# Attention and two expert layers on one core: mask added by TensorE, and three engines' order written by hand for the first two batches

## The chip, the cores and the metric

The kernel runs on one core of a Trainium2 chip. Times are device microseconds of one execution of the whole program. Of two times of this kernel that differ by under 0.3% (5.7 us) the measurement cannot say which is lower.

## What is computed

Three layers follow one another. Attention has 4 batches, 8 heads, 576 positions and head size 64; the first four heads see a band of 32 positions, the other four every fourth position of a band of 128. The second layer takes the larger of three products, and the third mixes eight experts with weights from a Sinkhorn iteration.

```
scores = scale * np.matmul(q, k.transpose(0, 1, 3, 2))
scores = np.where(masks[None, :, :, :], scores, -1000000000.0)
scores = scores - np.max(scores, axis=-1, keepdims=True)
attn = np.exp(scores)
attn = attn / (np.sum(attn, axis=-1, keepdims=True) + 1e-09)
x = np.matmul(attn, v)                      # then reshaped to (2304, 512)
h = np.maximum(np.maximum(x @ w1, x @ w2), x @ w3)
x = h @ w_out                               # second layer, d_ff 768
# third layer: 8 experts, each relu(x @ w1[e]) @ w2[e], weighted by P[:, e]
```

## The kernel before

**Work in units.** The second layer is computed batch by batch (b = 0 to 3) in tiles f of 128 hidden columns. One unit is 12 matmuls of 128x288 into one PSUM bank of a ring of four. A tile has six units: for each half of the batch's 576 positions the three products w1, w2, w3. After the first, ScalarE copies PSUM to `tmp`; after the second, VectorE takes the maximum with `tmp`; after the third it takes the maximum again, ScalarE writes the rounded half of `h` and VectorE the rest (a subtraction). Every product is done as three passes over such halves. The list `WORK` gives the order of tiles: batch 0's first five, then tiles 4 and 5 of batches 0 and 1 in turn (units 0 to 47), then `0.out`, the projection back (units 48 to 55), and so on. `hooks(unit)` is called after each unit and issues what goes beside it.

**Attention.** The four head pairs p of batch 0 come first, alone, by a list of steps, `ORDER`. A step's first letter says what it is: S scores (TensorE), M the mask and the maximum (VectorE), X the exponentials (ScalarE), R the reciprocal (VectorE) and the scaling with it (GpSimd), T transposes and E their evacuation, V the product with v, H and L the two halves of the result `xt`. `L290` is L, `L192` and `L200` are M. The pairs of batch 1 run beside units 0 to 29 of batch 0 (`BEGIN`, `STAGES`), those of batch 2 beside units 43 to 87.

**Weights' conversion.** The second layer's weights come as 64-bit floats and are turned to 32 bits by nine steps, c1 to c9 (`narrow_ops`): VectorE does c1, c3, c4, c6, c7 and c9, ScalarE c2, c5 and c8. Two chunks of 128x512 make a group g; c1 to c7 of a group are one instruction of 128x1024 each, c8 and c9 two of 128x512. Chunk j belongs to tile j // 3. Groups 0 and 1 are converted within the first part, groups 2 to 8 as the tiles need them, and groups 9 to 11 (the projection's) beside tiles 4 and 5.

**Who sets the order.** TensorE's instructions run in the order of the code throughout. On ScalarE, VectorE and GpSimd the list `ORDER` fixes the first part; from there to `1.out` the framework's scheduler orders them by its own estimates, so that several groups' steps may be interleaved; from `1.out` on ScalarE's and VectorE's order is the code's again. An engine runs its queue strictly in order: an instruction that waits holds all behind it.

Of the kernel before, what the change touches and what calls it, by code (L numbers as in the profile page):

```python
# [30 lines left out]
WEIGHTS = 78  # L31
# [14 lines left out]
FUSED = "1010"  # L46
EVAC = "AAV VAA VAV AAA".split()
ORDER = (
# [52 lines left out]
def attention_moe(ctx: ExitStack, tc: tile.TileContext, q, k, v, mask, wm1, wg, wm2, out):  # L101
# [27 lines left out]
    mk = at_p.tile([P, BANK0 + NQ * KW], F32, name="mk", bufs=1)  # L129
# [21 lines left out]
    def attn_ops(b, p, pool, qt, kt, vt, fused, evac):  # L151
# [12 lines left out]
        def s():  # L164
            if b == 0 and p % 2:
                h["s"] = [ps_g.tile([P, 512], F32, name="ps") for _ in range(2)]
            else:
                h["s"] = [ps_a.tile([P, 512], F32, name=f"pss{a}", bufs=1) for a in range(2)]

            for i in range(T0 if corners else 0):  # L170
                for a, (t0, t1) in enumerate(halves):
                    t = t0 + i
                    for j in range(2 if t < t1 else 0):
# [4 lines left out]
                            start=True, stop=True,  # L178
                        )
            for t in range(0 if corners else NQ):  # L180
# [3 lines left out]
                    start=True, stop=True,  # L184
                )

        def ma():
            h["m"] = pool.tile([P, NQ, KW], F32, name="sm", bufs=2 if pool is at_p else 3)
            for a, (t0, t1) in enumerate(halves):
                n = (t1 - t0) * KW  # L190
                m0 = BANK0 + t0 * KW if dil else a * KW
# [6 lines left out]
        def mb():  # L198
            h["st"] = pool.tile([P, 3, NQ], F32, name="st")
            nc.vector.tensor_reduce(out=h["st"][:, 0], in_=h["m"], axis=AX.X, op=ALU.max, negate=True)  # L200

        def xs():
            if not fused:
                nc.gpsimd.tensor_tensor(
                    out=h["m"], in0=h["m"], in1=h["st"][:, 0].unsqueeze(2).to_broadcast([P, NQ, KW]),
                    op=ALU.add,
                )

        def xe():
# [150 lines left out]
    def load_w1(b, g):  # L360
# [11 lines left out]
        if g < NG:  # L372
            nc.sync.dma_start(wm1f[g], raw)
# [1149 lines left out]
```

## Time and profile before

| | us |
|---|---|
| median of three runs | 1898.76 |
| lowest and highest | 1896.23, 1902.53 |
| the profiled execution's own time | 1901.93 |
| its span in the profile | 1899.9 |
| TensorE busy in the span | 1853.2 (98%) |
| VectorE, ScalarE, GpSimd busy | 1341.1, 976.6, 651.3 |

A share of the whole span says little here, since the change touches only the first fifth of it, up to about 342 us. Line numbers are those of the kernel before; `PE` is TensorE, `DVE` VectorE, `ACT` ScalarE, `POOL` GpSimd.

### The profile page before, as it was taken

What the parts mean: (1) busy time and instruction counts of PE and PEld (TensorE: products, weight loads), DVE (VectorE), ACT (ScalarE), POOL (GpSimd) and SP (SyncE); (2) the same over time, 40 slices, a digit from 0 to 9 for tenths busy, and PEclk for the clock granted to TensorE, in tenths of its full rate; (3) what the DMA queues carried; (4) which work ended last, traced back from release to release, by engine and by line L of the source; (5) the groups of instructions that cost most, each with busy time, mean ns of one, the idle gap of its engine ahead of it and who ended that gap; (6) DMA issues with size and microseconds to landing.
All of it is one profiled execution on the core that took longest, in us unless ns stands there. A gap on an engine that the chain in (4) does not pass through costs nothing.

```text
span 1899.9 us, 34083 instructions
## 1 busy us (share of the span) xinstructions
PE 1853.2 (98%) x12051; PEld 1745.9 (92%) x12051; DVE 1341.1 (71%) x2529; ACT 976.6 (51%) x2362; POOL 651.3 (34%) x553
## 2 busy tenths in 40 slices
PE   7899999999999999999999999999999999999998
PEld 6899999998899987999999999999989999999997
DVE  7983364677866667666677777777777677876777
ACT  5663445444554444444456555565545555555554
POOL 2123243335666667666612121121211111211111
PEclk7899999999999999999999999999999999999999
DMA  7766486866667678766977767777798676676763
GB/s 262 277 217 222 151 274 202 304 226 228 237 252 259 252 252 291 263 254 250 363 257 235 237 218 225 239 233 237 232 331 262 211 233 225 225 255 212 234 219 100
DMA packets 218488, 458.81 MB, mean 241 GB/s; under 512 B 19920, under 2 KB 102992, under 8 KB 216784
## 3 DMA queue, kind: packets, MB, share of 16 engines
q1 hardware_dynamic: 216688, 454.29, 70.2%
q10 hardware_dynamic: 1632, 2.36, 0.4%
q8 instruction: 95, 1.56, 0.3%
q14 instruction: 73, 0.60, 0.1%
HBM read 325.76 MB, written 130.81 MB: 240 GB/s over the span
## 4 chain that ended last, share of the span: by engine, by line
PE 83%; DVE 8%; DMA 4%; ACT 2%; issue 1%; POOL 1%; DVEq 0%; SPq 0%; ACTq 0%; POOLq 0%
PE po L1292 25%; PE po L1387 12%; PE po L1037 10%; PE ps L419 7%; PE p L1387 6%; PE q L1387 6%; PE q L1083 4%; PE p L1083 4%; PE ps L629 4%; DMA raw<-in_wm 1%; PE ps L549 1%; DVE sums L771 1%; PE q L549 1%; DVE h L1135 1%; DVE ts L810 1%
## 5 line engine op out<-in xcount | busy, mean ns | idle before, releaser
L1292 PE MATMUL po<-wt,hop 128*128 128x256 f32 (+1 forms) x3264 | 482.9, 310 | 2.8 <-DMA wt<-wtd 2.8
L1292 PEld LDWEIGHTS po<-wt,hop 128*128 128x128 f32 x3264 | 444.9, 191 | 38.5 <-ACT wt L83 3.0
L84 POOL TENSOR_TENSOR wt<-raw,wt 128x256 fp32r<-128x256 f32 x192 | 186.2, 994 | 757.9 <-ACT wt L83 746.9
L84 DVE TENSOR_TENSOR hop<-r,hop 128x384 fp32r<-128x384 f32 x384 | 208.9, 574 | 188.3 <-ACT hop L83 184.7
L1037 PE MATMUL po<-wb,h 128*128 128x512 f32 x1152 | 295.2, 392 | 0.4 <-POOL wb L84 0.4
L1037 PEld LDWEIGHTS po<-wb,h 128*128 128x128 f32 x1152 | 213.6, 188 | 34.3 <-POOL wb L84 1.2
L83 ACT CAST hop<-r 128x384 fp32r<-128x384 f32 x384 | 188.7, 516 | 55.7 <-DVE r L1268 30.8
L419 PE MATMUL ps<-xt,wa 128*128 128x288 f32 x1296 | 187.7, 301 | 4.6 <-DVE wa L323 2.0
L419 PEld LDWEIGHTS ps<-xt,wa 128*128 128x128 f32 x1296 | 176.9, 191 | 8.2 <-DVE wa L323 2.3
L84 POOL TENSOR_TENSOR wa<-raw,wa 128x256 fp32r<-128x256 f32 (+1 forms) x107 | 129.8, 1217 | 111.9 <-ACT wa L83 91.0
L1401 ACT ACTIVATE r<-r 128x384 f32<-128x384 f32 x192 | 99.8, 525 | 128.9 <-DVE r L1400 128.0
L84 POOL TENSOR_TENSOR tw<-ts,tw 128x512 fp32r<-128x512 f32 x64 | 85.3, 1354 | 93.5 <-DVE h L1135 57.4
L1387 PE MATMUL po<-xB,wa 128*128 128x384 f32 x576 | 116.9, 338 | 0.0
L1387 PE MATMUL po<-xt,wa 128*128 128x384 f32 x576 | 116.9, 338 | 0.0
L1321 DVE SCALAR_TENSOR_TENSOR acc<-po,prob,acc 128x256 f32<-128x256 f32 x222 | 95.1, 476 | 21.9 <-PE po L1292 17.5
L84 POOL TENSOR_TENSOR wa<-sums,wa 128x512 fp32r<-128x512 f32 x64 | 88.7, 1404 | 53.3 <-ACT wa L83 28.4
L84 POOL TENSOR_TENSOR wb<-raw,wb 128x512 fp32r<-128x512 f32 x64 | 93.2, 1456 | 29.2 <-ACT wb L83 28.8
L1387 PEld LDWEIGHTS po<-xB,wa 128*128 128x128 f32 x576 | 102.5, 188 | 0.0
L1387 PEld LDWEIGHTS po<-xt,wa 128*128 128x128 f32 x576 | 102.5, 188 | 0.0
L1262 DVE TENSOR_TENSOR r<-r,r 128x384 f32<-128x384 f32 x128 | 93.1, 728 | 2.2
L771 DVE TENSOR_TENSOR sums<-raw 128x256 f32<-128x256 f32 x64 | 41.4, 646 | 71.1 <-DMA raw<-in_wm 71.1
L1303 ACT COPY mm<-po 128x256 f32<-128x256 f32 x144 | 49.6, 375 | 79.9 <-PE po L1292 79.9
(236 smaller groups left out, 3364.7 us busy)
## 6 DMA issues: line engine op xcount, KB each, us to landing
wa<-wsd SPq DMA_DIRECT2D x192, 512.0 KB, 4.4
wt<-wtd SPq DMA_DIRECT2D x256, 256.0 KB, 3.9
wsd<-wa SPq DMA_DIRECT2D x96, 512.0 KB, 3.4
raw<-in_wm SPq DMA_DIRECT2D x64, 512.0 KB, 4.3
wtd<-tw SPq DMA_DIRECT2D x128, 256.0 KB, 2.8
raw<-in_wm SPq DMA_DIRECT2D x128, 256.0 KB, 5.4
wa<-wsd SPq DMA_DIRECT2D x64, 256.0 KB, 4.7
cx<-in_wm SPq DMA_DIRECT2D x12, 1024.0 KB, 6.8
```

The costliest lines, as they stand in the source:

```text
L83: nc.scalar.copy(hi, src)
L84: sub.tensor_tensor(out=lo, in0=src, in1=hi.bitcast(F32), op=ALU.subtract)
L419: nc.tensor.matmul(ps, w[:, wi, kk], xt[:, xi, kk, n0:n0 + HB], start=(n == 0), stop=(n == 3 * KT - 1),)
L629: nc.tensor.matmul(ps, wo[f][:, wi, d2 * P:(d2 + 1) * P], hs[f][:, hi, a * HB:(a + 1) * HB], start=(f == 0 and n == 0), stop=(f == NF1 - 1 ...
L771: nc.vector.tensor_tensor(out=s[:, o], in0=x, in1=y, op=op)
L1037: nc.tensor.matmul(po, self.hs[f, j][:, hi, t * P:(t + 1) * P], self.ws[f][:, wi], start=(n + f + k == 0), stop=(n == NPAIR - 1 and f == 1 ...
L1083: nc.tensor.matmul(ps, wo[w][:, wi, kk], xo[x][:, xi, kk], start=(first and k == 0), stop=True if k == 5 else False, skip_group_check=not ...
L1262: nc.vector.tensor_tensor(out=r[o, n], in0=r[x, n], in1=r[y, n], op=op)
L1292: nc.tensor.matmul(self.ps[side, t][:, 0:x.shape[-1]], h[:, hi, t * P:(t + 1) * P], x, start=(first and i == 0), stop=(n == NPAIR - 1 and ...
L1321: nc.vector.scalar_tensor_tensor(out=a, in0=src, scalar=g, in1=a, op0=ALU.mult, op1=ALU.add)
L1387: nc.tensor.matmul(ps[k][side], wo[k][w][:, wi, kk], xo[x][:, xi, kk], start=(first and c == 0), stop=c == 5, skip_group_check=not first,)
L1401: nc.scalar.activation(out=r, in_=r, func=AF.Relu)
```

## The change

In batches 0 and 1 a matmul writes the mask into PSUM first (`eyes`, an identity scaled by 8, times the mask's 64 rows), and the scores are added to it there. VectorE then takes only the maximum, straight from PSUM, and the exponentials read PSUM, with the scale and the maximum in the same instruction. Two pairs of batch 0 that had one long exponential with a subtraction on GpSimd and a sum on VectorE now have nine with their own sums, as the others. The first part has a new order of loads and steps and converts four chunks.

From there to `1.out` the scheduler no longer orders ScalarE, VectorE and GpSimd (`first.enter_context`): their queues hold what the code issues, unit by unit. A group's conversion is issued in four pieces beside four units, from the units in `NARROW` on: c1 c2, then c3 c4 c5, then c6 c7 c8, then c9. Batch 1's weights are split as batch 2's were, two units a chunk. Batch 1's and 2's attention steps are spread by new tables.

```diff
-OUTER = {"0.4": (0, 1), "0.5": (2,)}
-BEGIN = {1: (0, 5, 10, 16), 2: (43, 60, 67, 73), 3: (91, 98, 105, 112)}
+BEGIN = {1: (0, 6, 12, 17), 2: (43, 59, 66, 72), 3: (91, 98, 105, 112)}
-STAGES = {0: "S Ma Mb Xs Xe Xb Ra Rb", 6: "W", 8: "T0 E0 T1 E1", 9: "T2 E2", 11: "V0 H0 L0 V1 H1 L1"}
-LOADS = "k0 m0 k1 k2 m2 k3 v0 g0 v1 g1 v2 v3"
+SECOND = {
+    0: "S M", 1: "X0", 2: "X1", 3: "X2", 4: "X3 X4", 5: "Ra Rb", 6: "W",
+    8: "T0 E0 T1 E1", 9: "T2 E2", 10: "V0 H0", 11: "V1 H1 L0", 12: "L1",
+}
+NARROW = (0, 4, 8, 13, 17, 21, 25, 29, 33, 37)
+WEIGHTS = {1: 46, 2: 78}
+LOADS = "m0 k0 g0 w0 k1 m2 k2 k3 v0 g1 v1 v2 v3 g2"
-EVAC = "AAV VAA VAV AAA".split()
+EVAC = "VVV VVA AVA AVA".split()
...
+            for a, (t0, t1) in enumerate(halves if b < 2 else ()):
+                n, m0 = (t1 - t0) * KW, mask_at(a)
+                nc.tensor.matmul(
+                    h["s"][a][:, 0:n], eyes, mr[:QT, m0:m0 + n], start=True, stop=False, skip_group_check=True,
+                )
...
+        def m():
+            weights()
+            for a, (t0, t1) in enumerate(halves):
+                nc.vector.tensor_reduce(
+                    out=h["st"][:, 0, t0:t1],
+                    in_=h["s"][a][:, 0:(t1 - t0) * KW].rearrange("p (t k) -> p t k", k=KW),
+                    axis=AX.X, op=ALU.max, negate=True,
+                )
+            nc.vector.tensor_scalar_mul(h["st"][:, 0], h["st"][:, 0], 1.0 / D ** 0.5)
...
+    def narrow(g, step):
+
+        raw, ops = narrowing[g]
+        for name in ("c1 c2", "c3 c4 c5", "c6 c7", "")[step].split():
+            ops[name]()
+        if step == 2:
+            ws = [w1_tile(g) for _ in range(2)]
+            (made[0] if g < NG else wo).extend(ws)
+            parts = [(ws[i], raw[:, i]) for i in range(2)]
+            narrowing[g] = raw, parts
+            for w, x in parts:
+                nc.scalar.copy(w[:, 0], x)
+        if step == 3:
+            for w, x in ops:
+                nc.vector.tensor_tensor(out=w[:, 1], in0=x, in1=w[:, 0].bitcast(F32), op=ALU.subtract)
+            if g < NG:
+                nc.sync.dma_start(wm1f[g], raw)
...
+        for g, u in enumerate(NARROW, 2):
+            if 0 <= unit - u < 4:
+                narrow(g, unit - u)
+            if unit == max(u - 5, 0) and g > 2:
+                fetch_narrow(g)
...
+    first.enter_context(tc.manual_schedule(engines={EN.Activation, EN.DVE, EN.Pool}))
...
         if what == "1.out":
-            ordered.enter_context(tc.manual_schedule(engines={mybir.EngineType.Activation, mybir.EngineType.DVE}))
+            first.close()
+            ordered.enter_context(tc.manual_schedule(engines={EN.Activation, EN.DVE}))
```

Two places show what moves. The first is VectorE's queue where batch 0's first part ends and unit 0 follows; before, from the last products of attention on (L290 is L, L323 to L341 are conversion steps: L326 c1, L331 c3, L334 c4, L338 c6, L341 c7, L323 c9; numbers are those of buffers).

```order
L290 TENSOR_TENSOR xt_101<-ps_439,xt_101 128x112
L290 TENSOR_TENSOR xt_101<-ps_439,xt_101 128x144
L323 TENSOR_TENSOR wa_155<-raw_137,wa_155 128x512
L338 SCALAR_TENSOR_TENSOR cx_664<-cx_664 128x1024
L331 SCALAR_TENSOR_TENSOR raw_856<-cx_857,raw_856 128x1024
L323 TENSOR_TENSOR wa_478<-raw_137,wa_478 128x512
L341 TENSOR_TENSOR raw_663<-raw_663,cx_664 128x1024
L334 TENSOR_SCALAR cx_857<-cx_857 128x1024
```

After the change the same place of VectorE's queue (L305 is L; L214 and L219 are M of batch 1's first pair; L458 the maximum of unit 1; L347, L350, L354, L357 are c3, c4, c6, c7 of group 2, whose c1 stands further up):

```order
L305 TENSOR_TENSOR xt_105<-ps_479,xt_105 128x32
L214 TENSOR_REDUCE st_568<-pss0_545 128x5
L214 TENSOR_REDUCE st_568<-pss1_546 128x4
L219 TENSOR_SCALAR st_568<-st_568 128x9
L458 TENSOR_TENSOR tmp_521<-ps_572,tmp_521 128x288
L347 SCALAR_TENSOR_TENSOR raw_150<-cx_151,raw_150 128x1024
L350 TENSOR_SCALAR cx_151<-cx_151 128x1024
```

Groups 2 and 3 stood there interleaved with L; now M and a maximum stand ahead of group 2. The second place is VectorE's queue in the middle of batch 0's units, before (two and three groups at a time: buffers 873, 1064, 1220):

```order
L338 SCALAR_TENSOR_TENSOR cx_874<-cx_874 128x1024
L192 SCALAR_TENSOR_TENSOR sm_646<-pss1_627,mk_100 128x384
L192 SCALAR_TENSOR_TENSOR sm_646<-pss0_626,mk_100 128x480
L331 SCALAR_TENSOR_TENSOR raw_1064<-cx_1065,raw_1064 128x1024
L84 TENSOR_TENSOR h1_490<-ps_606,h1_490 128x288
L341 TENSOR_TENSOR raw_873<-raw_873,cx_874 128x1024
L326 TENSOR_SCALAR raw_1220<-cx_1221 128x1024
L200 TENSOR_REDUCE st_649<-sm_646 128x9
```

After the change VectorE's queue beside units 33 to 36, group 10 whole and the first step of group 11 (L343 c1, L398 c9, L463 the subtraction of a third unit):

```order
L343 TENSOR_SCALAR raw_1414<-cx_1415 128x1024
L458 TENSOR_TENSOR tmp_1511<-ps_1528,tmp_1511 128x288
L347 SCALAR_TENSOR_TENSOR raw_1414<-cx_1415,raw_1414 128x1024
L350 TENSOR_SCALAR cx_1415<-cx_1415 128x1024
L458 TENSOR_TENSOR ps_1545<-ps_1545,tmp_1511 128x288
L354 SCALAR_TENSOR_TENSOR cx_1415<-cx_1415 128x1024
L357 TENSOR_TENSOR raw_1414<-raw_1414,cx_1415 128x1024
L463 TENSOR_TENSOR hx_1451<-ps_1545,hx_1451 128x288
L398 TENSOR_TENSOR wb1_1562<-raw_1414,wb1_1562 128x512
L398 TENSOR_TENSOR wb1_1563<-raw_1414,wb1_1563 128x512
L458 TENSOR_TENSOR tmp_1568<-ps_1585,tmp_1568 128x288
L343 TENSOR_SCALAR raw_1507<-cx_1508 128x1024
```

One group is finished there before the next begins, and one operation of a unit stands between two steps.

## Rows read from the trace of the kernel before

**Rows 1.** Stretch, length, busy us (instructions) by engine; then clock, DMA share, GB/s.

```profile
0.00:47.50 47.50, 33.95 (x293) 29.73 (x293) 37.60 (x70) 27.12 (x77) 12.93 (x14) 0.78 0.77 262
47.50:118.70 71.20, 62.12 (x650) 58.32 (x649) 69.41 (x108) 50.19 (x144) 8.34 (x4) 0.93 0.71 255
118.70:151.90 33.20, 33.20 (x279) 32.71 (x277) 24.79 (x44) 16.69 (x49) 9.02 (x6) 1.00 0.71 247
151.90:342.40 190.50, 188.27 (x1816) 182.80 (x1816) 90.29 (x185) 84.68 (x282) 66.47 (x57) 1.00 0.64 211
```

**Rows 2.** TensorE in order of time: start, length, line, tiles, count, idle before.

```profile
47.50 1.86 PE L175 MATMUL pss<-kt,qt 64*64 64x96 f32 x36
...
118.68 25.70 PE L419 MATMUL ps<-xt,wa 128*128 128x288 f32 x192
144.31 1.04 PE L175 MATMUL pss<-kt,qt 64*64 64x96 f32 x36
...
151.87 3.31 PE L629 MATMUL ps<-h,wb 128*128 128x288 f32 x23
```

**Rows 3.** VectorE's groups by shape, 47.5 to 118.7 us: busy us, mean ns.

```profile
L338 DVE SCALAR_TENSOR_TENSOR cx<-cx 128x1024 f32<-128x1024 uint32 x8 | 11.9, 1487 | 0.2 <-ACT cx L337 0.2
L341 DVE TENSOR_TENSOR raw<-raw,cx 128x1024 f32<-128x1024 f32 x8 | 11.1, 1391 | 0.0
L323 DVE TENSOR_TENSOR wa<-raw,wa 128x512 fp32r<-128x512 f32 x15 | 9.9, 678 | 0.0
L331 DVE SCALAR_TENSOR_TENSOR raw<-cx,raw 128x1024 uint32<-128x1024 uint32 x8 | 9.7, 1211 | 0.0
L334 DVE TENSOR_SCALAR cx<-cx 128x1024 uint32<-128x1024 uint32 x8 | 5.5, 686 | 0.0
...
L200 DVE TENSOR_REDUCE st<-sm 128x9 f32<-128x864 f32 x4 | 4.2, 1042 | 0.0
...
L192 DVE SCALAR_TENSOR_TENSOR sm<-pss,mk 128x480 f32<-128x480 f32 x4 | 2.6, 644 | 0.0
L192 DVE SCALAR_TENSOR_TENSOR sm<-pss,mk 128x384 f32<-128x384 f32 x4 | 2.1, 534 | 0.0
...
L234 DVE TENSOR_SCALAR st<-st 128x9 f32<-128x9 f32 x4 | 0.7, 164 | 1.6 <-ACT sm L215 1.6
```

**Rows 4.** ScalarE's groups by shape in the same stretch.

```profile
L319 ACT CAST wa<-raw 128x512 fp32r<-128x512 f32 x15 | 8.6, 620 | 6.1 <-DVE raw L341 6.0
L337 ACT ACTIVATE cx<-cx 128x1024 f32<-128x1024 uint32 x7 | 8.2, 1173 | 0.0
L330 ACT ACTIVATE raw<-raw,ebias 128x1024 uint32<-128x1024 uint32 x7 | 8.2, 1165 | 0.1
```

**Rows 5.** VectorE in order of time, first steps of group 11.

```profile
132.06 0.68 DVE L326 TENSOR_SCALAR raw<-cx 128x1024 uint32<-128x1024 uint32 x1
132.66 0.45 DVE L84 TENSOR_TENSOR hx<-ps,hx 128x288 fp32r<-128x288 f32 x1
133.96 1.23 DVE L331 SCALAR_TENSOR_TENSOR raw<-cx,raw 128x1024 uint32<-128x1024 uint32 x1 [0.85 <-ACT raw L330]
```

**Rows 6.** VectorE in order of time, the first mask step, and conversion at 77 us.

```profile
7.07 0.66 DVE L192 SCALAR_TENSOR_TENSOR sm<-pss,mk 128x480 f32<-128x480 f32 x1 [6.07 <-PE pss L181]
...
77.18 1.22 DVE L338 SCALAR_TENSOR_TENSOR cx<-cx 128x1024 f32<-128x1024 uint32 x1
...
80.28 2.65 DVE L341 TENSOR_TENSOR raw<-raw,cx 128x1024 f32<-128x1024 f32 x1
```

**Rows 7.** GpSimd in order of time, one of four scalings between 60 and 112 us.

```profile
79.45 2.40 POOL L238 TENSOR_TENSOR sm<-sm,st 128x864 f32<-128x864 f32 x1 [15.24 <-ACT h L83]
```

**Rows 8.** Busy time and granted clock, three short stretches.

```profile
40.70:50.00 9.30, 6.38 (x51) 5.22 (x52) 9.30 (x17) 3.94 (x7) 0.00 (x0) 0.50 0.37 122
60.00:80.00 20.00, 16.84 (x179) 15.77 (x177) 20.00 (x35) 15.23 (x40) 2.45 (x2) 1.00 0.76 271
80.00:87.00 7.00, 4.53 (x19) 4.03 (x20) 7.00 (x8) 1.92 (x4) 1.85 (x1) 0.58 0.47 159
```

More of the change, by code (lines that the diff above doesn't have):

```diff
@@ L164, in s @@
         def s():
-            if b == 0 and p % 2:
+            if b == 0 and p in (1, 2):
                 h["s"] = [ps_g.tile([P, 512], F32, name="ps") for _ in range(2)]
@@ L177, in s @@
                             qt[r0:r0 + D, t, j * QT:(j + 1) * QT], kt[r0:r0 + D, t * QT:t * QT + KW],
-                            start=True, stop=True,
+                            start=b > 1, stop=True, skip_group_check=b < 2,
                         )
@@ L183, in s, with mask_at, weights, xe @@
                     qt[:, t], kt[:, t * QT:t * QT + KW],
-                    start=True, stop=True,
+                    start=False, stop=True, skip_group_check=True,
                 )
+        def mask_at(a):
+            return BANK0 + halves[a][0] * KW if dil else a * KW
+        def weights():
+            h["m"] = pool.tile([P, NQ, KW], F32, name="sm", bufs=2 if pool is at_p else 3)
+            h["st"] = pool.tile([P, 3, NQ], F32, name="st")
+        def m():
[7 more added lines that the diff above has]
+            nc.vector.tensor_scalar_mul(h["st"][:, 0], h["st"][:, 0], 1.0 / D ** 0.5)
+        def xe(t):
+            a = int(t >= T0)
+            c = (t - halves[a][0]) * KW
+            src, scale = (h["s"][a][:, c:c + KW], 1.0 / D ** 0.5) if b < 2 else (h["m"][:, t], 1.0)
+            nc.scalar.activation(
+                out=h["m"][:, t], in_=src, func=AF.Exp, scale=scale,
+                bias=h["st"][:, 0, t:t + 1], accum_out=h["st"][:, 1, t:t + 1],
+            )
+        def x(t0, t1):
+            for t in range(t0, t1):
+                xe(t)
         def ma():
-            h["m"] = pool.tile([P, NQ, KW], F32, name="sm", bufs=2 if pool is at_p else 3)
+            weights()
             for a, (t0, t1) in enumerate(halves):
-                n = (t1 - t0) * KW
-                m0 = BANK0 + t0 * KW if dil else a * KW
+                n, m0 = (t1 - t0) * KW, mask_at(a)
                 nc.vector.scalar_tensor_tensor(
@@ L390, in fetch @@
             return kept.pop(f)
-        if b == 2:
-            return made[b][3 * f:3 * f + 3]
-        ahead = 3 if b == 0 and f == NF1 - 2 else 0
-        while len(made[b]) < 3 * f + 3 + ahead:
-            made[b] += load_w1(b, len(made[b]) // 2)
         ws = made[b][3 * f:3 * f + 3]
@@ L714, in attention_moe @@
             m0, m1 = (0, BANK0) if i == 0 else (BANK0, BANK0 + NQ * KW)
-            nc.sync.dma_start(mk[:, m0:m1], mask[:, m0:m1])
-        else:
-            raws[i] = fetch_w1(0, i)
-    steps = {}
+            nc.sync.dma_start(mraw[:, m0:m1], mask[:QT, m0:m1])
+            if i == 0:
+                nc.scalar.copy(mr[:QT, m0:m1], mraw[:, m0:m1])
+        elif what[0] == "w":
+            nc.sync.dma_start(wgr, wg)
+        elif i < 2:
+            raws[i] = fetch_w1(0, i)
+        else:
+            fetch_narrow(i)
+    steps = {"r2": lambda: nc.gpsimd.tensor_copy(mr[:QT, BANK0:], mraw[:, BANK0:])}
     for p in range(H // 2):
-        fused = FUSED[p] == "1"
-        for name, op in attn_ops(0, p, pools[p], *qk[p], vs[p], fused, EVAC[p]).items():
-            if name not in ("W", "X0", "X1", "X2", "X3", "X4"):
+        for name, op in attn_ops(0, p, pools[p], *qk[p], vs[p], EVAC[p]).items():
+            if name not in "W X0 X1 X2 X3 X4 Ma Mb".split():
                 steps[f"{name[0]}{p}{name[1:]}"] = op
@@ L726, in attention_moe @@
     todo = ORDER.split()
-    for i in range(3):
+    for i in range(4):
         raw, t = raws[i // 2]
@@ L920, in hooks @@
             more_w1(0, what)
-        for late, step, op in ((0, 4, fetch_next), (4, 2, split_next)):
-            i, now = divmod(unit - WEIGHTS - late, step)
-            if 0 <= i < 36 // step and not now:
-                op(i)
+        for b, u in WEIGHTS.items():
+            for late, step, op in ((0, 4, fetch_next), (4, 2, split_next)):
+                i, now = divmod(unit - u - late, step)
+                if 0 <= i < (24, 36)[b - 1] // step and not now:
+                    op(b, i)
         for name in QUAD.get(unit, ()):
@@ L959, in attention_moe @@
             up(b, int(f), unit)
-            for g in OUTER.get(what, ()):
-                wo += load_w1(0, NG + g)
     fixed.close()
```

108 lines of the change are left out of this document (41 added, 67 removed), and 10 rows, old and new, of the table ORDER.

## The prediction

> **What bounds the kernel now.** I first cut the start of the program at the places where the work changes, and read each engine's busy time there [rows 1]. From 151.9 us on TensorE idles for 2.2 us of 190.5, and from 118.7 to 151.9 us not at all, so a reader should look ahead of 118.7 us. There VectorE is the full engine: 69.4 of 71.2 us, while TensorE is busy for 62.1 us, part of it at a lower granted clock (0.93 on the mean). Next I read TensorE in order of time [rows 2]. The first unit of the second layer ends when batch 1's first scores start, at 47.50 us. Batch 0's projection starts at 151.87 us. Sixteen units in one run took 25.70 us, so a unit is 1.61 us when nothing stops it, and from 118.68 us on nothing did. The change can move the 47.50 and the 151.87; what follows the second shifts with it.
>
> Then I read what fills VectorE: by its groups, 48 of the 69 us are the five costliest conversion steps [rows 3]. ScalarE's conversion steps of the same stretch are in [rows 4].
>
> **What the change takes from VectorE.** A pair's mask and maximum were 0.64 + 0.53 + 1.04 = 2.21 us [rows 3]. A maximum straight from PSUM is not in the trace. The nearest rows are the mask steps, with the same PSUM elements, 1.17 us for both; with a multiply on 9 columns (0.16 us, the last of [rows 3]) it is 1.33 us, so 0.9 us less a pair. (From below: 1.04, as if PSUM were as quick as SBUF; from above 2.21, no gain.)
>
> *First part.* VectorE was busy for 37.6 us up to 47.5 [rows 1]. Less four pairs' 0.9 (3.6), two sums of 864 columns that go (2 x 1.04 = 2.1), and the steps of groups 2 and 3 that stood there and now don't (c1, c3, c4, c6: 0.69 + 1.21 + 0.69 + 1.22 = 3.8). More by three evacuations of 384 columns from PSUM (as the mask step on 384, 0.53 each) and one c9 (0.68): 2.3. That leaves 30.4. Before it lie 7.1 us in which the first load and scores are awaited [rows 6]; mask and scores still need those. For waits within I take 5 us (before: 37.6 of 40.4 after the first step, so 2.8 of waiting; now strictly in one order with more ScalarE work between, at most 8). First unit done: 7.1 + 30.4 + 5 = **42.5 us**, 5.0 earlier; bounds 40.5 and 45.5.
>
> *To group 2.* Behind the last L, VectorE's queue has batch 1's first maximum, then the maximum of unit 1, then c3 of group 2. The first waits for the scores behind unit 0, the second for unit 1, and all conversion is queued behind both. The granted clock was 0.50 from 40.7 to 50 us [rows 8], at which those scores took 1.86 us against 1.04 [rows 2] and a unit takes twice 1.61. Two mask matmuls of 864 columns together are not in the trace; by the 288 columns in 0.134 us (1.61 / 12) they are 0.4 us, 0.8 at that clock; nothing at best, as they may run while TensorE waits. So 0.8 + 1.9 + 3.2 + 0.45 = **6.4 us** to c3, at 48.9; 3.5 if the clock is up.
>
> **What it adds: groups one behind the other.** This is the step on which the forecast rests. A group's nine steps depend on each other, and its engine changes six times. In front of each of VectorE's steps its queue now waits for ScalarE's, because no other group's step stands between; before, two or three groups were mixed and VectorE had no idle time in front of such steps [rows 3]. Where only one group was left, the old kernel shows the wait: c3 of group 11 started 1.90 us after c1, with 0.85 us idle though a subtraction stood between [rows 5]. One group in series: c1 0.68, c2 1.17, c3 1.21, c4 0.69, c5 1.17, c6 1.22, c7 1.22, first c8 0.62, two c9 1.36 = 9.34 us [rows 3 to 5]; the next c1 follows 0.08 sooner than the last c9's end (0.60 from start to start against 0.68 [rows 5]), so **9.3 us**. From c3 of group 2: 9.3 - 1.9 = 7.4, then groups 3 to 11, nine times 9.3 = 83.7. Sum 91.1.
>
> Between one group's c9 and the next c1 stand ten maxima or subtractions (0.45 each, 0.37 from start to start), one pair's maximum (1.2), one reciprocal (0.4), and seven L pieces priced as a maximum is but partly shorter (2.1): 7.4 us. Within groups, what does not fit under the waits for ScalarE: pair 1's maximum behind c7 (0.7), two waits for the last exponentials of a pair (0.6 and 0.5), pair 3's maximum with reciprocal ahead of c3 (1.7), exponentials ahead of c2 on ScalarE (0.8), L behind c7 (0.4): 4.7, none at best.
>
> GpSimd's four scalings of batch 1 stay. While one ran (79.45, 2.40 us) c7 took 2.65 us, and c6 without it 1.22 [rows 6, 7]; I take 2.0 us for two such hits, since the others fall into waits or on operations from PSUM; bounds 0 and 4 x 1.43 = 5.7. The Trainium skill (SBUF — State Buffer, "Who interferes with whom") has VectorE and GpSimd exclude each other for whole instructions where VectorE reads two SBUF operands, and never in a reduction from PSUM. The 1.43 us here agrees; by that rule alone all four could hit, and the sum would be 3.7 higher.
>
> Sum: 42.5 + 6.4 + 91.1 + 7.4 + 4.7 + 2.0 = 154.1 us for c9 of group 11, beside unit 40. TensorE cannot run free before that, since each bank of its ring of four comes back through the same VectorE queue; its units then take 9.5 / 4 = 2.4 us and not 1.61. Then unit 41's maximum, copy and subtraction (1.2) free a bank, and units 45 to 47 remain (4.8): **160.1** against 151.87, so 8.2 us later. The projection's weights are done by then. Loads I cost at nothing, since a group's is issued four or five units, some 10 us, ahead of its c1. So are batch 1's splits, now later, on GpSimd: from 151.9 us on it is busy for 66 of 190 us [rows 1]. If that cover is too thin, TensorE waits there and the sum is too low. The profiled execution's 1901.9 becomes 1910.1; its own time lies 3.2 us above the median, so the prediction is 1898.8 + 8.2 = **1907.0**.
>
> **Rivals.** *Faster: the waits are covered.* If ScalarE's step were always done when VectorE comes to it, VectorE's own work sets the pace. The waits that I count between 42.5 and 154.1 us are some 26: about 2.0 a group in ten groups, and 6.4 at the start. Without them VectorE is done at 128, and TensorE's own work decides: 47 units x 1.61 = 75.7; for four pairs' scores, transposes and products what its 62.1 us hold beside 27 units, 18.6; 1.0 for batch 2's scores and 1.6 for masks; 97 us, so 139.4 and a time of 1886. It decides from 8.2 of the 26 us on; with half of them covered it is 1894. For it speaks that a unit's operation stands in nearly every wait; against it [rows 5], where one did and 0.85 us were left.
>
> *No change.* The clock is up at unit 0 (2.9 less), scalings hit nothing (2.0), and pairs fit under the waits (half of 4.7): 8.2 - 7.2 = +1.0, 1899.8.
>
> *Slower still: TensorE's clock.* It is fed 1.61 of every 2.4 us. Busy for 16.8 of 20 us it kept the full 2.4 GHz; in 80 to 87 us, after a stop of 4.5 us, it had 0.58 [rows 8]. At 1.2 GHz a unit is 3.2 us, 0.8 above the pace; over units 29 to 40 that is 9.6 us, and I'd take half: 1912. The Trainium skill (TensorE: Matmul & The Clock Gate, "A second HAM failure mode: psum-queue depth-cycling") tells of a clock that swings when TensorE idles briefly between groups of matmuls; by that rule all of it, 1916.6. Rows with 84% busy do not show it; no row here has 67% for long.
>
> **How the numbers follow.** Waits in series as summed: 0.36; with the falling clock 0.14; no change 0.32; covered 0.18. Slower by over 0.3% (above 1904.5) takes the first two, 0.50; within 0.32; faster 0.18. For the likeliest alone the unknown costs give 8.2 - 2 - 2.9 - 2 - 2.4 and 8.2 + 3 + 3.7: 1898 to 1914. The range for all reaches into the covered case as far as half of it and up to the falling clock: 1891 to 1916.
>
> **What would show it.** Right: VectorE idles for 20 us or more between 43 and 155 us, released by ScalarE's c2, c5 and c8; c1 to c1 of groups 9 to 11 is 9.4 to 10 us; scores of batch 1's first pair start near 42.5; the projection starts near 160. Wrong: that VectorE stays over 90% busy there, or that the first part ends before 39 us or after 47, or that TensorE waits later for splits of batch 1.

## The result, and the profile after

The changed kernel takes 1921.01 us (median of 4 runs, 1918.53 to 1924.34), and the kernel before, run beside it, 1899.11 (1896.23 to 1902.53): ratio 1.0116, 95% interval 1.0093 to 1.0139. The forecast was 1907.0 with a range up to 1916: the sign was right, the size less than half of what came. The profiled execution took 1921.69, with a span of 1919.9.

The same four stretches as in [rows 1], of the kernel after:

```profile
0.00:47.50 47.50, 32.51 (x246) 27.72 (x246) 26.68 (x56) 23.77 (x94) 8.41 (x11) 0.75 0.88 270
47.50:118.70 71.20, 59.50 (x590) 53.37 (x589) 54.60 (x97) 41.93 (x133) 4.90 (x3) 0.93 0.57 193
118.70:151.90 33.20, 29.29 (x250) 27.55 (x248) 27.08 (x47) 16.85 (x34) 2.10 (x2) 1.00 0.64 214
151.90:342.40 190.50, 186.50 (x1787) 180.31 (x1786) 93.38 (x192) 89.92 (x302) 67.05 (x57) 0.99 0.65 217
```

In the second, VectorE was busy for 54.6 us where it had been for 69.4, and TensorE for 59.5 where it had been for 62.1. In the same stretch of time all engines did less: they waited more. TensorE in order of time, where [rows 2] had 47.50 and 151.87:

```profile
52.34 0.53 PE L450 MATMUL ps<-xt,wa 128*128 128x288 f32 x2 [0.66 <-DVE xt L305]
52.80 0.66 PE L184 MATMUL pss<-mk,eyes 64*128 64x480 f32 x2
53.39 1.04 PE L192 MATMUL pss<-kt,qt 64*64 64x96 f32 x36
...
172.70 3.48 PE L655 MATMUL ps<-h,wb 128*128 128x288 f32 x25
```

Unit 0 ends 5.3 us later, and the projection starts 20.8 us later; the span grew by 20.0, so all but 0.8 us of the loss lies ahead of the projection. What lies between the two I call the stretch: 104.4 us before, 119.9 now. Here it is before and after, read as the rows above:

```profile
47.50:151.87 104.37, 95.29 (x926) 91.00 (x925) 94.17 (x151) 66.85 (x191) 17.32 (x10) 0.95 0.71 253
52.80:172.70 119.90, 102.67 (x933) 94.94 (x933) 93.12 (x152) 64.97 (x178) 7.72 (x6) 0.94 0.55 183
```

VectorE's work in it is the same (94.2 and 93.1 busy us); its idle time went from 10.2 to 26.8 us, TensorE's from 9.1 to 17.2. Who was waited for, 47 to 172 us of the kernel after (us in total, times, longest):

```profile
DVE cx L354 <- ACT cx L353: 6.1, 8, 0.9
DVE raw L347 <- ACT raw L346: 4.2, 6, 0.9
DVE st L214 <- POOL sm L253: 3.0, 2, 1.8
...
PE pst L264 <- ACT pt L268: 7.2, 4, 3.7
PE pss L184 <- ACT sm L225: 3.0, 3, 2.4
...
ACT cx L353 <- DVE cx L350: 15.3, 9, 4.3
ACT wa L395 <- DVE raw L357: 13.4, 7, 3.0
ACT raw L346 <- DVE raw L343: 7.8, 6, 3.8
ACT wb L395 <- DVE raw L357: 7.1, 3, 2.6
```

VectorE waits for ScalarE's conversion steps (12.5 us with c8's; 2.2 before), ScalarE for VectorE's (43.6 us; 11.8 before), and TensorE for ScalarE, in front of transposes whose bank isn't evacuated and of masks whose bank is still read by exponentials (10.2 us; 0.6 before). VectorE waits for no load there, ScalarE once for 2.0 us. How the waits hang together is seen around 111 us. ScalarE stands at c8 until VectorE has done c7, the evacuation comes behind it, and TensorE's transposes wait for that:

```profile
111.20 1.14 ACT L395 CAST wa<-raw 128x512 fp32r<-128x512 f32 x2 [1.93 <-DVE raw L357]
...
113.17 0.85 ACT L268 COPY pt<-pst 96x384 f32<-96x384 f32 x2
...
113.70 0.53 PE L264 MATMUL pst<-ident,sm 128*96 128x128 f32 x3 [3.69 <-ACT pt L268]
```

One whole group in order of time on ScalarE:

```profile
138.22 1.15 ACT L346 ACTIVATE raw<-raw,ebias 128x1024 uint32<-128x1024 uint32 x1 [0.19 <-DVE raw L343]
139.40 0.40 ACT L456 COPY tmp<-ps 128x288 f32<-128x288 f32 x1
141.40 1.13 ACT L353 ACTIVATE cx<-cx 128x1024 f32<-128x1024 uint32 x1 [1.59 <-DVE cx L350]
145.08 1.14 ACT L395 CAST wb<-raw 128x512 fp32r<-128x512 f32 x2 [2.55 <-DVE raw L357]
146.13 0.39 ACT L460 CAST hx<-ps 128x288 fp32r<-128x288 f32 x1
```

and the same group on VectorE, from its c1 to the next group's:

```profile
137.51 0.68 DVE L343 TENSOR_SCALAR raw<-cx 128x1024 uint32<-128x1024 uint32 x1
...
139.41 1.23 DVE L347 SCALAR_TENSOR_TENSOR raw<-cx,raw 128x1024 uint32<-128x1024 uint32 x1 [0.27 <-ACT raw L346]
...
142.56 1.23 DVE L354 SCALAR_TENSOR_TENSOR cx<-cx 128x1024 f32<-128x1024 uint32 x1 [0.84 <-ACT cx L353]
...
145.74 1.29 DVE L398 TENSOR_TENSOR wb<-raw,wb 128x512 fp32r<-128x512 f32 x2 [0.31 <-ACT wb L395]
...
147.31 0.68 DVE L343 TENSOR_SCALAR raw<-cx 128x1024 uint32<-128x1024 uint32 x1
```

Each of the two stands until the other is through, and what is queued behind a standing step, such as the unit's cast at 146.13 us, stands with it.

### The profile page after: what moved, and what is told of

It reads as the page before. It is cut to its first block, busy times and chain, and to the rows that moved or that the text cites. A ratio compares the mean times of both kernels' runs of the same rounds, so it can differ in the third digit from the quotient of the medians.

```text
span 1919.9 us, 34148 instructions
## 1 busy us (share of the span) xinstructions
PE 1863.4 (97%) x12061; PEld 1750.7 (91%) x12061; DVE 1327.5 (69%) x2532; ACT 977.9 (51%) x2394; POOL 643.1 (33%) x552
## 4 chain that ended last, share of the span: by engine, by line
PE 80%; DVE 9%; DMA 5%; ACT 3%; issue 2%; POOL 1%; SPq 0%; DVEq 0%; POOLq 0%; ACTq 0%
PE po L1326 24%; PE po L1421 12%; PE po L1071 9%; PE p L1421 6%; PE q L1421 6%; PE ps L450 6%; PE p L1117 4%; PE q L1117 4%; PE ps L655 4%; PE ps L575 1%; PE q L575 1%; DMA raw<-in_wm 1%; DMA cx<-in_wm 1%; DVE h L1169 1%; DVE ts L837 1%
## 5 line engine op out<-in xcount | busy, mean ns | idle before, releaser
L1355 DVE SCALAR_TENSOR_TENSOR acc<-po,prob,acc 128x256 f32<-128x256 f32 x222 | 95.0, 475 | 21.3 <-PE po L1326 17.5
L1296 DVE TENSOR_TENSOR r<-r,r 128x384 f32<-128x384 f32 x128 | 93.1, 727 | 2.2
```

Of the source, the lines that this page charges most:

```text
L1296: nc.vector.tensor_tensor(out=r[o, n], in0=r[x, n], in1=r[y, n], op=op)
L1355: nc.vector.scalar_tensor_tensor(out=a, in0=src, scalar=g, in1=a, op0=ALU.mult, op1=ALU.add)
```

## The experiments

For all: the time against runs of the kernel before on the same chip, and from the profiled execution, one of each version, the end of unit 0, the start of the projection and the stretch between.

| run | ratio to before (95%) | unit 0 ends | projection | stretch |
|---|---|---|---|---|
| before | 1 | 47.50 | 151.87 | 104.4 |
| the change | 1.0116 (1.0093–1.0139) | 52.80 | 172.70 | 119.9 |
| no early c1 | 1.0103 (1.0090–1.0116) | 47.70 | 171.42 | 123.7 |
| scheduler | 1.0066 (1.0053–1.0078) | 54.32 | 160.88 | 106.6 |
| pairs of groups | 1.0153 (1.0138–1.0167) | 48.02 | 179.18 | 131.2 |
| old start | 1.0101 (1.0088–1.0114) | 46.09 | 171.77 | 125.7 |
| staggered | 1.0144 (1.0129–1.0160) | 49.66 | 176.92 | 127.3 |
| without c2, c5 | 1.0050 (1.0034–1.0067) | 49.66 | 160.51 | 110.9 |
| staggered, `st` x2 | 1.0119 (1.0102–1.0136) | 46.25 | 173.07 | 126.8 |
| spread | 1.0077 (1.0065–1.0090) | 51.43 | 163.73 | 112.3 |
| spread, `st` x2 | 1.0056 (1.0043–1.0068) | 48.19 | 160.08 | 111.9 |
| hand order, ScalarE only | 1.0145 (1.0122–1.0169) | 50.41 | 173.09 | 122.7 |
| hand order, VectorE only | 1.0174 (1.0160–1.0188) | 50.01 | 178.64 | 128.6 |
| masks alone | 1.0064 (1.0052–1.0077) | 53.41 | 164.35 | 110.9 |
| loads first | 1.0070 (1.0057–1.0082) | 48.90 | 161.38 | 112.5 |
| spread, VectorE's masks | 1.0047 (1.0035–1.0059) | 47.17 | 160.01 | 112.8 |
| turns apart | 1.0016 (1.0007–1.0025) | 47.07 | 153.60 | 106.5 |
| turns apart, VectorE's masks | 1.0027 (1.0016–1.0038) | 47.25 | 154.24 | 107.0 |
| turns apart, pair 1 later | 1.0048 (1.0029–1.0066) | 47.68 | 158.64 | 111.0 |
| turns apart, early c1 | 1.0017 (1.0005–1.0030) | 47.89 | 152.37 | 104.5 |

Two cautions for reading it. What lies behind the projection differs between these executions too, by up to some 7 us (with the scheduler 1754.8 us, before 1748.0), so a projection and a ratio need not move together. And TensorE's granted clock differs. Reckoned from the granted clock of short pieces of the stretch, TensorE was at 1.2 GHz for 9.8 us of it before, 13.6 in the change, 20.5 in no early c1, 27.4 in the old start, 23.9 staggered, 10.2 spread, 20.9 with the masks alone and 6.8 with turns apart, and at 2.4 GHz for the rest. Ten us at half speed are at most 5 us of work; a difference of that size between two stretches can be the clock's and need not be a wait.

**The first part.** In the first part's queue of VectorE stood, ahead of group 1's c3, the c1 of group 2; in the profiled execution of the change it waited for its load:

```profile
36.36 0.69 DVE L343 TENSOR_SCALAR raw<-cx 128x1024 uint32<-128x1024 uint32 x1 [3.84 <-DMA cx<-in_wm]
36.97 0.69 DVE L347 SCALAR_TENSOR_TENSOR raw<-cx,raw 128x512 uint32<-128x512 uint32 x1
```

No early c1:

```diff
-NARROW = (0, 4, 8, 13, 17, 21, 25, 29, 33, 37)
+NARROW = (1, 4, 8, 13, 17, 21, 25, 29, 33, 37)
```

> Group 2's conversion starts beside unit 1 and no longer beside unit 0, so that its c1 no longer stands in VectorE's queue ahead of group 1's c3 (where it waited 3.84 us for its load). Theory A (that wait holds all that stands behind it in the first part): unit 0 ends 2.5 to 4 us earlier than 52.8, at 49 to 50.3; group 2's c1 and c2 then come behind, 1.9 us, so the projection starts 0.5 to 2.5 us earlier than 172.7. Rival B (the first part is late because its first loads are late and by ScalarE's work): unit 0 ends at 52 to 53, the projection at 172 to 175.

Unit 0 ended 5.1 us earlier, more than theory A asked, and the projection 1.3; the time stood (1920.74). Of the lead 3.8 us were lost behind it: TensorE idled 2.6 us more in the stretch and was busy 1.2 us longer for the same work, at the lower clock. The old start is a second test of this: the kernel before up to the end of its first part, VectorE's masks throughout, and behind it the change's pieces and order.

```diff
-            for g in OUTER.get(what, ()):
-                wo += load_w1(0, NG + g)
...
+        for g, u in enumerate(NARROW, 2):
+            if 0 <= unit - u < 4:
+                narrow(g, unit - u)
...
+    first.enter_context(tc.manual_schedule(engines={EN.Activation, EN.DVE, EN.Pool}))
```

> The kernel before up to the end of its first part, with VectorE's masks and its loads, and the changed kernel's order by hand, pieces and starts of conversion behind it. Theory A (the order by hand costs what the stretch behind unit 0 grew by, 15 us, the start the other 5): unit 0 ends at 47 to 49 as before, the projection starts at 164 to 169, time 12 to 17 us over before. Rival B (masks by TensorE and the late start are the cause, and the hand order costs nothing by itself): projection at 152 to 156, time within 4 us of before.

Unit 0 ended at 46.09, the projection started at 171.77, and the time was 1918.89 against 1900.48. Rival B falls. Theory A has the cause, but with 18.4 us the order cost more than the 12 to 17 it gave. So neither the late start nor TensorE's masks are needed for the loss; the hand order with its pieces suffices. Its price is less certain: up to 8.8 us of this stretch's extra 21.3 can be the lower clock (27.4 us against 9.8).

**Whose order.** The scheduler again, behind the first part:

```diff
-    first.enter_context(tc.manual_schedule(engines={EN.Activation, EN.DVE, EN.Pool}))
```

> The changed kernel with the orders of ScalarE, VectorE and GpSimd again left to the scheduler behind the first part; masks, pieces and loads as changed. Theory A (nine steps of a group in series, VectorE waiting for ScalarE's step and nothing else allowed past): from unit 0's end to the projection 105 to 112 us in place of 119.9, the projection at 157 to 165, time 8 to 15 us under the changed kernel's. Rival B (the pace is set by where the steps are written in the program, or by VectorE's work): within 3 us of the changed kernel.

The stretch fell by 13.3 us, as theory A had it, and the time by 8.4 us; unit 0 ended 1.5 us later in that execution. The kernel stays 0.66% over before. Kept for one engine alone (`engines={EN.Activation}`, `engines={EN.DVE}`):

> The changed kernel with the order by hand kept for ScalarE alone behind the first part; VectorE's and GpSimd's are the scheduler's. Theory C (ScalarE's fixed queue is what blocks): the time stays within 3 us of the changed kernel. Theory A (VectorE's fixed queue is): most of the 8.4 us that the scheduler gave back on all engines comes back.

> The order by hand kept for VectorE alone; ScalarE's and GpSimd's are the scheduler's. Theory C: 5 us or more of the 8.4 us come back. Theory A: within 3 us of the changed kernel.

With one engine fixed nothing comes back. With VectorE alone the time is longer than with all fixed (1931.2), against both theories. With ScalarE alone it is 1926.6, against theory A, and 5.6 us from the changed kernel where theory C allowed 3, with intervals that overlap. The loss is no one engine's. That a free engine's order doesn't fit a fixed one's would explain it; no run shows it.

**Is it VectorE's series?** Pairs of groups:

```diff
-NARROW = (0, 4, 8, 13, 17, 21, 25, 29, 33, 37)
+NARROW = (1, 3, 8, 10, 16, 18, 24, 26, 32, 34)
```

> Still one order by hand, but groups start in pairs two units apart (1, 3, 8, 10, 16, 18, 24, 26, 32, 34), so that a step of the other group stands between the steps of one. Theory A (series of one group): VectorE's waits for ScalarE in front of c3, c6 and c9 fall from about 2 us a group to under 1, the stretch from unit 0's end to the projection is 8 to 12 us shorter than 119.9. Rival B (VectorE's own work and GpSimd's port set the pace): 116 to 121 us, waits only move.

Wrong for both: 9 us slower. VectorE's waits moved to TensorE's products, perhaps because units without conversion now run between units with two groups:

```profile
DVE tmp L458 <- PE ps L450: 12.9, 7, 3.5
DVE cx L354 <- ACT cx L353: 5.9, 8, 0.9
DVE ps L458 <- PE ps L450: 4.7, 4, 1.7
...
PE pst L264 <- ACT pt L268: 10.6, 4, 6.5
PE pss L184 <- ACT sm L225: 7.6, 4, 3.3
```

Staggered pieces, and without ScalarE's steps:

```diff
-            if 0 <= unit - u < 4:
-                narrow(g, unit - u)
+            when = (u - 2, u, u + 2, u + 4) if g > 2 else (u, u + 1, u + 2, u + 3)
+            if unit in when:
+                narrow(g, when.index(unit))
```
```diff
-        for name in ("c1 c2", "c3 c4 c5", "c6 c7", "")[step].split():
+        for name in ("c1", "c3 c4", "c6 c7", "")[step].split():
```

> The changed kernel with the four pieces of groups 3 to 11 two units apart instead of one (the first two units earlier, the last one later, the group's load two units earlier), the younger group first, so that a step of another group, or two units' operations, stand in VectorE's queue between a step and the ScalarE step that it needs. Same operations, still one order by hand. Theory A (a group's steps in series are what costs): VectorE's waits for ScalarE's conversion steps behind unit 0 fall from 12.5 us to under 5, the stretch from unit 0's end to the projection from 119.9 to 107 to 113, the time by 6 to 12 us. Rival B (the pace is set by TensorE's and ScalarE's waits for each other at batch 1's pairs, as pairs of groups made nothing better): waits move, stretch 117 to 122, time within 3 us of the changed kernel.

> ScalarE's two steps c2 and c5 of groups 2 to 11 are left out, so the weights made are not the reference's; VectorE keeps all of its steps. Theory A: 2.3 us of ScalarE and the waits around them go from each of ten groups' series, stretch 119.9 to 102 to 108. Rival B (VectorE's own work of 93 us with batch 1's pairs set the pace): 114 us or more.

The staggering did what it was to do to VectorE's waits (of 12.5 us 0.6 are left), and the kernel got 6 us slower: theory A, which is my prediction's, falls as a full account. The clock cannot save it. Its 10.3 us more at the lower level are at most 5.2 of this stretch of 127.3, which would leave 122.1, far from the 107 to 113 asked. ScalarE's own waits had not shrunk (45.1 us), and VectorE's came back behind TensorE:

```profile
DVE ps L458 <- PE ps L450: 6.6, 4, 2.6
DVE tmp L458 <- PE ps L450: 6.5, 4, 3.5
...
DVE cx L354 <- ACT cx L353: 0.3, 1, 0.3
...
PE pst L264 <- ACT pt L268: 8.0, 3, 3.7
...
ACT cx L353 <- DVE cx L350: 23.6, 10, 5.3
```

Without c2 and c5 the stretch was 110.9, between what the theories asked: 9 of the 15.5 us that the stretch had grown by hang on ScalarE's two steps and the waits around them. With two buffers for `st` (a pair's small sums), and no early c1, beside the staggering:

```diff
-            h["st"] = pool.tile([P, 3, NQ], F32, name="st")
+            h["st"] = pool.tile([P, 3, NQ], F32, name="st", bufs=2)
```

> The staggered pieces, and besides group 2's conversion beside unit 1 (no c1 waiting for its load in the first part) and two buffers for a pair's small sums (a maximum of batch 1 then does not wait for GpSimd's scaling of the pair before, 3.0 us). Theory A: unit 0 ends at 47 to 49, the stretch is 105 to 112, the time 3 to 6 us under that with staggered pieces alone. Rival C (an earlier start is given back behind, as it was when only the start was moved): within 2 us of staggered pieces alone.

The time was 6.0 us under staggered alone, so at the end of the 3 to 6 that theory A gave for this pair of edits; but its stretch, 126.8, was nowhere near the 105 to 112 that should have come with it.

**Both queues at once.** The spread order gives each change of engine, ScalarE's steps too, a unit of its own:

```diff
-        for name in ("c1 c2", "c3 c4 c5", "c6 c7", "")[step].split():
+        for name in ("c1", "c2", "c3 c4", "c5", "c6 c7", "", "")[step].split():
...
+            elif 0 <= unit - u + 3 < 7:
+                narrow(g, unit - u + 3)
```

> One order by hand, every step of groups 3 to 11 in a unit of its own: c1, then c2 one unit later, c3 c4, c5, c6 c7, c8, c9, starting three units before the changed kernel's c1 and so ending as there. With staggered pieces VectorE had stopped waiting for ScalarE's conversion steps (0.6 us) but ScalarE still waited 45 us for VectorE's, with copies, exponentials and evacuations of batch 1 queued behind, and the time did not fall. Theory C (ScalarE's queue, blocked by a conversion step whose input isn't made, is what holds TensorE and then VectorE): ScalarE's waits for conversion steps fall under 20 us, TensorE's waits for ScalarE (12 us) under 6, the stretch from unit 0's end to the projection to 107 to 114. Rival D (a fixed interleaving of three engines by units costs this whatever stands next to what, since the work per unit is uneven and TensorE is at most four banks ahead): stretch 117 or more, waits of VectorE for TensorE stay above 10 us.

> The same with group 2's conversion beside unit 1 and two buffers for a pair's small sums, as was tried with the staggered pieces. Theory C: 2 to 6 us under the spread order alone. Rival D: unit 0 ends 3 to 5 us earlier, and 3 us or less of it is left at the projection.

Theory C: ScalarE's waits for conversion steps fell from 43.6 to 15.2 us, the stretch to 112.3, the time by 7.5 us, and by 12.1 with the other two edits. From the spread order:

```profile
ACT cx L353 <- DVE cx L350: 9.5, 5, 4.9
...
ACT wb L396 <- DVE raw L357: 2.9, 2, 1.7
ACT wa L396 <- DVE raw L357: 2.8, 3, 1.2
...
PE pst L264 <- ACT pt L268: 5.6, 2, 3.1
```

ScalarE doesn't idle much less: its waits for VectorE's maxima, in front of the units' casts, rose from 5.1 to 22.8 us. Not all of theory C held either: TensorE's waits for ScalarE were still 7.6 us, and 9.2 with the other two edits, and VectorE's for TensorE 10.2, which theory D had said. Of the 9.2, 4.5 stood in front of transposes, and these were set apart (`SECOND`):

```diff
-    8: "T0 E0 T1 E1", 9: "T2 E2", 10: "V0 H0", 11: "V1 H1 L0", 12: "L1",
+    7: "T0 E0", 8: "T1 E1", 9: "T2 E2", 10: "V0 H0", 11: "V1 H1 L0", 12: "L1",
```

> The spread order with two buffers and no early c1, with the first three transposes of a pair of batch 1 one unit earlier than the second, so that ScalarE's evacuation of the first is behind when the third needs its bank. Theory C: TensorE's wait for the evacuations falls from 4.5 us to under 2, time 1 to 3 us under 1908.9. Rival D: the wait moves on, within 1.5 us.

The wait for the evacuations went from 4.5 us to 0.2, and the stretch from 111.9 to 106.5, in 1904.0 us. That is more than the 1 to 3 us of theory C; TensorE was at 1.2 GHz for 6.8 us of this stretch and for 13.7 of the one that it is measured against, which can be up to 3.4. TensorE's waits of this kernel, 47 to 160 us:

```profile
PE pss L184 <- ACT sm L225: 5.8, 3, 3.9
PE ps L451 <- DVE xt L305: 2.3, 2, 1.6
PE pst L264 <- POOL sm L253: 0.9, 1, 0.9
```

**What the masks on TensorE are worth.** First alone in the kernel before (batch 1 only):

```diff
+            for a, (t0, t1) in enumerate(halves if b == 1 else ()):
...
+        if b == 1:
+            ops.update(Ma=m, Mb=list, Xe=xm)
```

> The kernel before with one part of the change alone: batch 1's four masks by TensorE, maximum and exponentials straight from PSUM; batch 0, the loads, the weights' conversion and all orders as before, but for GpSimd's copy of the masks into TensorE's format. Theory E (VectorE is full there and loses 0.9 us a pair): 2 to 4 us under before, since four pairs' work goes from the full engine. Rival F (what VectorE saves is given back, since the banks of the scores are now held until ScalarE's last exponential and TensorE waits there with the next pair's mask): within 2 us of before, or up to 3 over.

Then taken out of the spread kernel with two buffers, and out of turns apart:

```diff
-            for a, (t0, t1) in enumerate(halves if b < 2 else ()):
+            for a, (t0, t1) in enumerate(() if b else halves):
...
-    0: "S M", 1: "X0", 2: "X1", 3: "X2", 4: "X3 X4", 5: "Ra Rb", 6: "W",
+    0: "S Ma Mb", 1: "X0", 2: "X1", 3: "X2", 4: "X3 X4", 5: "Ra Rb", 6: "W",
```

> The spread order with two buffers and no early c1, and batch 1's masks again by VectorE with the exponentials from SBUF; batch 0's stay with TensorE, and the order of all else is the same by hand, so that the price of batch 1's masks on TensorE stands alone (with the masks alone put on TensorE the scheduler had also drawn another c1 in front of a wait in the first part, and half of the 12.5 us lay there). Theory E (0.9 us of VectorE a pair is worth it): 2 to 5 us slower than with TensorE's masks, 1911 to 1914. Rival F (score banks held until the last exponential, mask matmuls of 0.5 us a pair): VectorE's 3.6 us fit into its waits for TensorE, TensorE's wait of 4.7 us for the exponentials goes, time 1905 to 1909.

> Turns apart, and batch 1's masks by VectorE as before: with the transposes' wait gone, TensorE's longest wait is 5.4 us in front of pair 1's mask, whose banks are held until ScalarE's last exponential. Rival F (the held banks are the price of TensorE's masks): that wait goes, VectorE's 3.6 us more fit into its waits, 1 to 5 us under turns apart alone. Theory E (VectorE's work counts now that TensorE waits less): 1 to 4 us over it.

In the first both expectations failed: 12.5 us slower. 5.9 of the projection's 12.5 us lay in the first part, where the scheduler had drawn a c1 ahead of a pair's reciprocal, on VectorE:

```profile
27.55 0.43 DVE L361 TENSOR_SCALAR raw<-cx 128x512 uint32<-128x512 uint32 x1 [4.14 <-DMA cx<-in_wm]
27.89 0.21 DVE L268 RECIPROCAL st<-st 128x9 f32<-128x9 f32 x1
```

The other 6.5 lay in the stretch:

```profile
53.41:164.35 110.94, 102.03 (x933) 95.97 (x933) 90.38 (x149) 64.80 (x188) 17.34 (x10) 0.91 0.65 228
```

VectorE was relieved as forecast, from 94.2 to 90.4 us, and TensorE idled no more than before (8.9 us against 9.1). But TensorE was busy for 6.7 us more. The mask matmuls took 4.5 of these, about 1.1 a pair, and the rest came with the lower clock (20.9 us against 9.8). TensorE had been as full as VectorE there, so the work had gone from one full engine to another.

In fixed orders the intervals overlap: 1.0056 with, 1.0047 without; 1.0016 with, 1.0027 without. There batch 1's masks on TensorE neither gain nor cost what can be measured here, and neither theory E nor F is borne out.

**What is left.** Pair 1 a unit later, loads and conversion of group 0 behind pair 1, and the early c1 put back (`NARROW` from 0):

```diff
-BEGIN = {1: (0, 6, 12, 17), 2: (43, 59, 66, 72), 3: (91, 98, 105, 112)}
+BEGIN = {1: (0, 7, 12, 17), 2: (43, 59, 66, 72), 3: (91, 98, 105, 112)}
```
```diff
-LOADS = "m0 k0 g0 w0 k1 m2 k2 k3 v0 g1 v1 v2 v3 g2"
+LOADS = "m0 k0 k1 m2 g0 k2 w0 k3 v0 g1 v1 v2 v3 g2"
```

> Turns apart with batch 1's pair 1 begun one unit later (7 in place of 6), masks by TensorE: its mask matmul then comes 1.6 us or more later behind pair 0's exponentials. Rival F: the wait of 5.4 us falls to under 3.5, time 1 to 3 us under turns apart alone. If the time does not move, what TensorE waits there is made up behind.

> The spread order with two buffers and no early c1, and in the first part pair 1's queries and keys loaded ahead of group 0 with the conversion of group 0 behind pair 1's maximum in all orders. Theory G (the first part is late because TensorE waits 5 us for pair 1's load): scores of pair 1 start 3 to 5 us earlier, unit 0 ends 1.5 to 4 us earlier than 48.2, the time 1 to 3 us under the spread order with two buffers. Rival H (VectorE's and ScalarE's order behind it sets the first part's end): unit 0 ends at 47.5 to 49, time within 1.5 us.

> Turns apart with group 2's conversion again beside unit 0, so that its c1 stands in the first part's queue ahead of group 1's c3; nothing else is changed. Theory J (a later end of the first part reaches the projection once the stretch behind it is near TensorE's own work): unit 0 ends 2 to 5 us later than 47.1, the projection 2 to 5 us later than 153.6, the time 1905.5 to 1909. Rival (an end of the first part that is a few us later is made up behind, as in the changed kernel): time within 1.5 us of turns apart.

In the first, the held banks' wait fell to 0.7 us, and waits of 4.2 us for GpSimd's scalings took its place; the time rose (1907.8) where rival F had it fall. With pair 1's load first, pair 1's scores started 2.2 us earlier, but unit 0 ended at 48.90 and not earlier, as theory H had it; the time was 0.14% above that of the spread order with two buffers, more than its 1.5 us, with intervals that overlap. In the last run's profiled execution the early c1 waited 0.5 us for its load, unit 0 ended 0.8 us later, and the time stood. So that run doesn't test theory J. No version beat the kernel before; turns apart is nearest, 0.16% over it by 11 runs against 16, with an interval that leaves out 1.

## Why the prediction was wrong

**The sum, step by step.** To the end of unit 0 it had 42.5 us and 52.8 were measured; from there to c3 of group 2, 6.4 and 3.9; from there to c9 of group 11, 105.2 and 110.0; from there to the projection, 6.0 and 6.0. Two steps failed: the waits of the first part, and the claim that behind it VectorE's queue alone makes the pace.

**VectorE's saving: right.** A pair's maximum from PSUM was priced at 1.33 us. It took 0.66, 0.55 and 0.17, 1.38 together. First part's work, 30.4 forecast, was 31.0.

**The first part, 42.5: the step that failed by most.** It took 52.8 in the profiled execution. The 5 us of waits, "at most 8", were 13.7: from the first maximum (7.62) to the last L's end (52.28) are 44.7 us less 31.0 busy. 4.8 are loads, which I had costed at nothing: the order showed c1 of group 2 in this queue (3.8 of them), and I priced only loads issued units ahead. 4.6 are scores that TensorE, itself waiting 5.0 us for pair 1's load, had not made, and 2.4 are transposes. Other executions of the same first part ended at 49.66 to 51.43. But the runs also showed that this step can't simply be added to the next: 5.1 us off it gave 1.3 us at the projection and 0.3 us of the time. From the end of unit 0 to the projection the sum had 117.6 us; it was 119.9 in the change, but 123.7 and 125.7 where unit 0 ended at 47.70 and 46.09, with more of it at the lower clock.

**To group 2: too high.** 3.9 us and not 6.4, since the clock was up from 46.8 us.

**Groups in series: the pace right, the cause half.** Forecast 9.4 to 10 us from c1 to c1; they stand at 137.51, 147.31 and 157.12. VectorE's idle time of over 20 us is there (22.9 from c3 of group 2 to c9 of group 11). But the sum had about 20 of it, 2.0 a group, in front of steps that wait for ScalarE's conversion, and these were 12.5; the others were waits that the sum had at nothing: 4.1 for TensorE's products, 3.0 for GpSimd and 2.1 behind an evacuation on ScalarE. That the pace came out right is in part luck. What failed is the claim that VectorE's queue alone makes the pace, and so that the parts of the sum add up: with its waits for ScalarE gone nothing was gained (staggered). I had counted no wait of TensorE in the stretch beyond its ring; it waited 10.2 us for ScalarE, which stood at conversion steps. When these steps and the evacuations were moved apart, the stretch fell from 119.9 to 106.5 us.

**GpSimd's scalings: right in number.** Two of the four lay on a step c6, which took 1.98 and 1.77 us in place of 1.23: 1.3 us of the 2.0 forecast. At the other two VectorE stood waiting for the scaling itself.

**Rivals.** The covered waits and no change didn't come. The falling clock was not the cause of this kernel's loss: from 52.8 us on TensorE had 1.2 GHz for 13.6 us, before for 9.8 (3.0 from 47.5 on, then 81.2 to 88). The 3.8 us more are at most 2 us of work. The three falls:

```profile
67.30:74.10 6.80, 6.36 (x53) 5.81 (x54) 6.13 (x9) 3.01 (x8) 1.63 (x1) 0.50 0.46 155
115.10:118.50 3.40, 3.40 (x30) 3.01 (x29) 2.02 (x3) 2.24 (x8) 0.00 (x0) 0.51 0.91 287
156.00:159.40 3.40, 3.40 (x16) 3.40 (x15) 2.51 (x6) 1.76 (x4) 0.00 (x0) 0.50 0.44 149
```

The Trainium skill (TensorE: Matmul & The Clock Gate, "A second HAM failure mode: psum-queue depth-cycling") tells of a clock that swings when TensorE idles briefly between groups of matmuls. The trace agrees with a swing, in these three falls, but not with the forecast's reading of it, all of units 29 to 40 at the lower clock: TensorE ran them from 133.9 to about 159 us, and only the last of the falls, from 156.0 on, touches them.

**Signs named.** "The first part ends after 47": it came, and named the first step. Of the signs of being right the pace and the idle time came, the scores near 42.5 and the projection near 160 did not. Scalings by GpSimd cost in a way that I hadn't listed, 3.0 us of VectorE's maxima that wait until the scaling before has read the small sums.

What stays open: how much of the first part's lateness reaches the end in a median execution, since its loads and clock differ from one execution to the next by more than the edits did; how much of a stretch is TensorE's lower clock and how much waiting, beyond the bounds given; and the 0.16% that turns apart still has over before.

## What to carry over

When an order is fixed by hand over several engines that feed each other, place each engine's step at least one unit behind the step that it needs, on every one of them: in this kernel, removing one queue's waits while the other still stood only moved them. Count for each fixed queue what stands behind a waiting step and who waits for that, TensorE too, before adding up the chain of the engine that looks full. And test an added order apart from the work that it comes with: in the same hand order the masks moved off VectorE changed nothing that could be measured, and with the scheduler in place of the hand order the stretch was 13.3 us and the time 8.4 us shorter. Look at the engine that work is moved to as well: TensorE was as full as VectorE.

## What the runs showed of the hardware

An exponential of 96 columns from PSUM took 0.341 us on the mean in the changed kernel's stretch, against 0.364 from SBUF:

```profile
L225 ACT ACTIVATE sm<-pss,st 128x96 f32<-128x96 f32 x36 | 11.9, 341 | 0.2 <-DVE st L219 0.2
...
L225 ACT ACTIVATE sm<-sm,st 128x96 f32<-128x96 f32 x4 | 1.5, 364 | 0.2 <-DVE st L245 0.2
```

The same first part, whose instructions are the same, ended between 49.66 and 52.80 us in different profiled executions; in the slowest, 281 GB/s were moved from 5 to 47.5 us, in the others 299 to 306.

TensorE's granted clock fell after stops, and how long it stayed at 1.2 GHz in the stretch went from 6.8 to 27.4 us between versions with the same matmuls but for eight masks. In the change, TensorE stopped for 2.4 us up to 67.7, for 3.7 us up to 113.7 and for 3.2 us up to 155.3, and the clock was down from 67.3, 115.1 and 156.0 on.
